# Batch 0's layers and the second attention, laid out step by step by a planner with its own list of durations

## The chip, the core and the metric

The kernel runs on one core of a Trainium2 chip. A core has a matrix engine (TensorE; PE in the profile, its weight loads PEld), VectorE (DVE), ScalarE (ACT), GpSimd (POOL), and SyncE (SP), which here only issues DMAs. Each engine works through its own list of instructions in order and waits on semaphores for the others. The metric is the device time of one execution in microseconds (us), the median over several.

## The reference

Linear attention over 4 batches of 8 heads, 576 positions, 64 dimensions, followed by two feed-forward networks on the 2304 x 512 result:

```python
def phi(x):                                   # x: q or k, w_phi: 64 x 128
    proj = np.einsum('bhsd,df->bhsf', x, w_phi)
    proj = proj - np.max(np.abs(proj), axis=-1, keepdims=True)
    return np.concatenate([np.exp(proj), np.exp(-proj)], axis=-1)
kv = np.einsum('bhsf,bhsd->bhfd', phi(k), v)
num = np.einsum('bhsf,bhfd->bhsd', phi(q), kv)
den = np.einsum('bhsf,bhf->bhs', phi(q), phi(k).sum(axis=2))[..., None] + 1e-06
x = (num / den) laid out as 2304 x 512
h = x @ w_in;  x = np.maximum(0.01 * h, h) @ w_out          # 512 -> 2048 -> 512
g = x @ w_gate                                              # 512 -> 1536
y = (g / (1 + np.exp(-g)) * (x @ w_val)) @ w_out2           # 1536 -> 512
```

The weights come in as 64-bit floats.

## The kernel before

A batch is 576 tokens, worked on as two halves of 288 columns. A layer is cut into *units*: an L1 unit makes 128 of the 2048 hidden rows ("1", f), a gate or val unit 128 of the 1536 ("g", f and "v", f), an out unit adds four such blocks into one of four 128-row blocks of the result. Every product is taken as three matmuls, since an operand is split in a high part and a low rest: (xh, wi high), (xl, wi high), (xh, wi low) at L821 (`in_ops`), and the same with gp and wo at L869 (`u_out`). All of them are recorded at L816 (`products`). A half of an input unit is 12 matmuls.

Each weight block of 128 x 512 passes through a chain the first time it is needed: a 512 KB DMA of the 64-bit words into a wi tile (L675), on ScalarE the magnitude (L691), the low bits (L694) and, for some, the sign (L697), on VectorE the shift and sign (L701, or L707 and L711) and the rounding (L719), which gives 32-bit floats in wr. These are stored to DRAM for the later batches (kept<-wr, L725). Then ScalarE rounds the high part into a wi or wo tile (L737) and VectorE subtracts the rest (L78). From batch 1 on, wr<-kept loads replace the chain's first part. There are 5 wi, 5 wo, 4 wr, 5 gp and 4 pm buffers.

An opening (the list OPENING, L41) writes batch 0's attention and the first weights out as one fixed order. After it, batch 0's units run in the order of `units`; weights are taken ahead by `split_next` (L1228), and the steps of batch 1's attention are strewn between the units by `spread` (L1242). There the tile scheduler sets the order on each engine; instructions stamped with one token keep their order. Key steps of an attention: kT load (raw, L155), projection (L207), largest (L212), two exponentials (L218, L219), product with the values (L248). Query steps: qT load, split into high and low (pk, L90 and L78), projection (L366, L367), column maxima (L370), turn (L388), the row of maxima (L394 to L406), its subtraction on PE (L420), two exponentials (L430, L436), the product with kv (L459), the denominator (L465), its reciprocal (L476 to L484) and the division (L492). Batch 2's keys go through a split of their own (pk<-raw) before their projection.

## Time and profile before

| | |
|---|---|
| three runs | 1053.72, 1054.14 (median), 1057.67 us |
| profiled execution | 1054.82 us, of which the span of its instructions 1052.9 us |
| busy in the span | PE 98%, PEld 97%, DVE 75%, ACT 62%, POOL 2% |
| granted clock of TensorE | 1.00 in every stretch shown (2.4 GHz) |
| opening | up to about 51 us |
| batch 0's layers with batch 1's attention | about 51 to 321 us |

An engine's line in a view gives its instructions' own durations; two neighbours overlap in part, so what an instruction holds its engine for is the step from its start to the next one's start. The ends of matmuls are modelled. A wait is shown in brackets behind the instruction that ended it, with the engine and line it waited for.

### The profile page before, as it was taken

How to read it: one execution, taken by the hardware profiler on the slowest of the kernel's cores; microseconds unless marked ns; L12 is line 12 of the kernel's file. 1: busy time of each engine (PE TensorE's matmuls, PEld its weight loads, DVE VectorE, ACT ScalarE, POOL GpSimd, SP SyncE). 2: the span in 40 equal slices, each digit the busy share in tenths (PEclk: the TensorE clock that was granted, in tenths of full speed). 3: DMA queues.
4: the chain of work that ended last, by engine and by line, in shares of the span. 5: the costliest groups of instructions: out<-in, count | busy, mean ns of one | idle time of the engine just before them, and what ended most of it. 6: DMA issues, size and time to landing. Idle time of an engine off the chain costs nothing.

```text
span 1052.9 us, 20402 instructions
## 1 busy us (share of the span) xinstructions
PE 1036.7 (98%) x7638; PEld 1016.8 (97%) x7638; DVE 793.5 (75%) x1726; ACT 650.5 (62%) x1448; POOL 21.4 (2%) x57
## 2 busy tenths in 40 slices
PE   9999999999999999999999999999999999999998
PEld 7899999999999999999999989999999999999998
DVE  6988888998999799678676766868778632468464
ACT  6879887898977788456543667735443244336431
POOL 1001100000000000000000000000000000000000
PEclk9999999999999999999999999999999999999999
DMA  8239777577765998765535486356886777558542
GB/s 267 60 129 309 274 264 263 168 248 217 261 192 200 356 339 284 285 230 192 192 120 189 134 319 243 141 203 217 291 285 237 272 267 264 183 167 297 191 145 76
DMA packets 101489, 236.16 MB, mean 224 GB/s; under 512 B 19856, under 2 KB 35984, under 8 KB 101392
## 3 DMA queue, kind: packets, MB, share of 16 engines
q1 hardware_dynamic: 95888, 219.74, 60.3%
q0 software_dynamic: 4032, 14.68, 3.6%
q8 instruction: 60, 0.98, 0.4%
q10 hardware_dynamic: 1472, 0.46, 0.2%
q14 instruction: 37, 0.30, 0.1%
HBM read 169.30 MB, written 65.54 MB: 223 GB/s over the span
## 4 chain that ended last, share of the span: by engine, by line
PE 83%; DVE 6%; ACT 5%; DMA 4%; issue 1%; SPq 0%; POOL 0%; DVEq 0%; ACTq 0%; POOLq 0%
PE pm L816 55%; PE pa L942 9%; PE pm L942 5%; PE pa L459 5%; PE pa L248 2%; PE pa L260 2%; PE pa L207 2%; DMA wi<-in_w_dram 2%; ACT wr L691 1%; DMA wr<-kept 1%; ACT wi L694 1%; ACT gp L90 1%; DVE gp L78 1%; PE pm L518 1%; DVE wr L701 1%
## 5 line engine op out<-in xcount | busy, mean ns | idle before, releaser
L816 PE MATMUL pm<-xh,wi 128*128 128x288 f32 x1664 | 350.5, 298 | 1.4 <-ACT wi L737 1.2
L816 PE MATMUL pm<-gp,wo 128*128 128x288 f32 x2256 | 338.4, 296 | 2.8 <-DVE acc L883 2.3
L816 PEld LDWEIGHTS pm<-gp,wo 128*128 128x128 f32 x2256 | 311.9, 188 | 4.8 <-DVE acc L883 3.0
L816 PEld LDWEIGHTS pm<-xh,wi 128*128 128x128 f32 x1664 | 271.1, 188 | 3.2 <-ACT wi L737 1.4
L816 PE MATMUL pm<-xl,wi 128*128 128x288 f32 x832 | 246.2, 297 | 0.0
L816 PEld LDWEIGHTS pm<-xl,wi 128*128 128x128 f32 x832 | 156.1, 188 | 0.8
L883 DVE TENSOR_TENSOR acc<-pm,acc 128x288 f32<-128x288 f32 x160 | 70.0, 452 | 47.2 <-PE pm L816 46.4
L78 DVE TENSOR_TENSOR gp<-es,gp 128x576 fp32r<-128x576 f32 x94 | 70.6, 752 | 31.8 <-ACT gp L90 31.0
L90 ACT ACTIVATE gp<-es 128x576 fp32r<-128x576 f32 x94 | 64.8, 694 | 29.9 <-DVE es L864 24.9
L78 DVE TENSOR_TENSOR wi<-wr,wi 128x512 fp32r<-128x512 f32 x96 | 64.7, 683 | 12.1 <-ACT wi L737 11.5
L737 ACT ACTIVATE wi<-wr 128x512 fp32r<-128x512 f32 x92 | 58.0, 643 | 25.6 <-PE pm L816 10.8
L942 PE MATMUL pm<-xh,wi 128*128 128x288 f32 x272 | 62.6, 297 | 1.8 <-DMA wi<-parts 1.6
L78 DVE TENSOR_TENSOR fl<-ff,fh 128x512 fp32r<-128x512 f32 (+1 forms) x72 | 50.9, 712 | 12.1 <-ACT fh L90 11.8
L691 ACT ACTIVATE wr<-wi 128x512 f32<-128x512 f32 x68 | 47.9, 704 | 17.0 <-DMA wi<-in_w_dram 7.8
L719 DVE TENSOR_TENSOR wr<-wr,wi 128x512 uint16<-128x512 uint16 x68 | 51.1, 754 | 0.8
L942 PEld LDWEIGHTS pm<-xh,wi 128*128 128x128 f32 x272 | 46.3, 188 | 2.9 <-DMA wi<-parts 1.8
L694 ACT ACTIVATE wi<-wi 128x512 int32<-128x512 uint32 x68 | 47.8, 703 | 0.0
L90 ACT ACTIVATE fh<-ff 128x512 fp32r<-128x512 f32 (+1 forms) x72 | 47.2, 665 | 0.8
L844 ACT ACTIVATE es<-pm 128x288 f32<-128x288 f32 x72 | 29.8, 431 | 25.4 <-PE pm L942 15.9
L465 ACT ACTIVATE dn<-pa 64x288 f32<-64x288 f32 x64 | 26.0, 407 | 30.5 <-PE pa L459 29.5
L90 ACT ACTIVATE acc<-pm 128x288 f32<-128x288 f32 x64 | 26.7, 433 | 26.3 <-PE pm L816 26.0
L864 DVE SCALAR_TENSOR_TENSOR es<-pm,es 128x288 f32<-128x288 f32 x72 | 32.1, 449 | 14.3 <-PE pm L816 14.1
(214 smaller groups left out, 2068.0 us busy)
## 6 DMA issues: line engine op xcount, KB each, us to landing
wo<-parts SPq DMA_DIRECT2D x77, 512.0 KB, 6.2
wi<-parts SPq DMA_DIRECT2D x68, 512.0 KB, 5.6
parts<-wi SPq DMA_DIRECT2D x56, 512.0 KB, 4.9
wi<-in_w_dram SPq DMA_DIRECT2D x44, 512.0 KB, 5.0
wr<-kept SPq DMA_DIRECT2D x64, 256.0 KB, 4.8
parts<-wo POOLq DMA_DIRECT2D x28, 512.0 KB, 5.2
kept<-wr SPq DMA_DIRECT2D x40, 256.0 KB, 4.5
wi<-in_wg_dram SPq DMA_DIRECT2D x12, 512.0 KB, 4.6
```

The costliest lines, as they stand in the source:

```text
L78: keep(dve.tensor_tensor(out=o, in0=a, in1=b, op=ALU.subtract))
L90: keep(act.activation(o, a, AF.Copy))
L459: keep(pe.matmul(ps, w, x, start=(i == 0), stop=(i == len(ops) - 1)))
L691: after_opening(act.activation(t[0], high.bitcast(F32), AF.Abs, scale=REBIAS))
L694: after_opening(act.activation(low, low.bitcast(U32), AF.Copy, scale=2.0**-29))
L719: keep(dve.tensor_tensor(out=t16, in0=t16, in1=e16, op=ALU.add))
L737: i = act.activation(t[:, 0], r, AF.Copy)
L816: m = pe.matmul(ps, w, x[:, c], start=(i == 0), stop=(i == n - 1))
L844: act.activation(o, i, AF.Prelu, alpha=0.01)
L864: dve.scalar_tensor_tensor(out=g[:, c], in0=ps, scalar=0.5, in1=g[:, c], op0=ALU.mult, op1=ALU.mult)
L883: dve.tensor_tensor(out=acc[o][:, t], in0=ps, in1=acc[o][:, t], op=ALU.add)
L942: m = pe.matmul(ps, a, b, start=start and n == 0, stop=stop and n == 5, skip_group_check=True)
```

## The change

A planner is added. `plan()` makes one job for each step of batch 0's units 0 to 59, of the weight chains that they need, and of batch 1's whole attention; also for the opening's last steps (TAIL, cut off OPENING), the stores kept<-wr, and the loads. A job has a cost name, the jobs it needs, the buffers it takes and uses, and a due time that follows from PE's order. `lay_out` is a list scheduler: due times are handed back from the last job to the first, then each engine takes, of the jobs that can begin first, the one due first. COSTS holds for each step how long it occupies its engine and when its result is there; a load is counted at 330 GB/s, behind the loads before it, and 1.9 us more. The jobs are emitted in that order and stamped with the opening's token. Units 60 to 63 (gate and val 10 and 11) and all behind them are left to the old way; their four weight blocks are converted in the plan without a due time of their own and stay in wi tiles.

The weights of L1, gate and val in the plan go to fh and fl tiles (3 of each) instead of wi. The split of the constants (wbd, wst), which stood beside the opening, becomes two planned jobs. `w_load` beyond those of the plan begins after unit 60. The arithmetic is the same and so are the counts of the instructions of each engine, but for the order.

```diff
+COSTS = {
+    "PE": {
+        "KP": (0.43, 0.60), "KB": (0.88, 1.05), "QP": (0.27, 0.43), "QT": (0.08, 0.30), "QS": (0.13, 0.30),
...
+    "SP": {"LD": (0.42, 1.9)},
...
+SIGNAL, RATE, FAR = 0.08, 330.0, 1.0e9
...
+def lay_out(jobs, clocks, slots, live, stay):
...
+        if j.engine in ("DVE", "ACT"):
+            j.due = min(j.due, begin.get(j.engine, FAR) - j.hold)
+            begin[j.engine] = j.due
...
+            first = min(t for t, _ in can)
+            t, j = min((c for c in can if c[0] <= first + 0.03), key=lambda c: c[1].due)
+            for u, k in can:
+                if u < t + j.hold and k.due < min(j.due, u + k.hold):
+                    t, j = u, k
...
+        if j.size:
+            moved = max(moved, t + j.hold) + j.size / RATE / 1e3
+            j.end = moved + j.result
...
-    def split_constants():
-        again = T([P, 2, F], F32, "es", 5)
-        nc.sync.dma_start(out=again.rearrange("p h f -> p (h f)"), in_=w_phi)
-        dve.tensor_copy(wbd_h, again)
...
     def parts_tile(key):
+        if in_plan[0] and key[0] in "1gv" and key not in used_later:
+            wtile[key] = t = T([P, 512], F32R, "fh", 3), T([P, 512], F32R, "fl", 3)
+            return t
...
+    UP = bounds[0][2] - 4
+    first_keys = [k for i in range(-1, UP) for k in slots[i]]
+    used_later.update(k for i in range(UP, UP + 4) for k in need[i])
...
+            ld = job("LD", call(w_load, key), [later(conv_of[first_keys[n - 5]] if n > 4 else None), round_by.get(n - 5)], [("wi", r)], size=524288)
+            ca = job("CA", call(step, 0), [ld] + [low_by[m] for m in [n - 4] if m in low_by], [("wr", w)], [r])
...
+            if kind in "1gv":
+                job("LD", call(store_f32, key), [cf], (), [w], size=262144)
...
+        nextk = job("LD", call(load_k, 2, 0), [later(qn_of[2 * NP - 1, 1])], [("raw", ("k", 2, 0))], size=294912 + 327680)
...
+        for i in range(UP):
+            for j in pes[i]:
+                j.due, now = now, now + j.hold
+            for j in at.get(i, []):
+                j.due, now = min(j.due, now), now + j.hold
...
-    for b in range(B - 1):
+    for b in range(1, B - 1):
         first, mid, end = bounds[b]
-        if b == 0:
-            mid -= 4
...
-    conv[0] = done[0] = 4
-    split_constants()
-    opening[0] = False
-    for i in range(NU):
+    in_plan[0] = True
+    for j in plan():
+        j.fn()
+    opening[0] = in_plan[0] = False
+    loaded[0] = conv[0] = done[0] = len(first_keys)
+    for i in range(UP, NU):
```

Three places show how the order moves. The first is VectorE's list ahead of the last of the four groups of out units behind batch 0's L1 (the additions acc<-pm at L883, which free pm banks for PE). Before:

```order
L701 SCALAR_TENSOR_TENSOR wr_2494<-wr_2494,wi_2299 128x512
L78 TENSOR_TENSOR wi_2445<-wr_2392,wi_2445 128x512
L719 TENSOR_TENSOR wr_2494<-wr_2494,wi_2299 128x512
L370 TENSOR_REDUCE cst_sb<-pa_2567 128x9
L701 SCALAR_TENSOR_TENSOR wr_2539<-wr_2539,wi_2346 128x512
L883 TENSOR_TENSOR acc_1068<-pm_2360,acc_1068 128x288
L883 TENSOR_TENSOR acc_1068<-pm_2374,acc_1068 128x288
```

And of the change, at the same additions (there L1473, with L865 the rounding, L847 the shift and sign, L202 the subtraction):

```order
L847 SCALAR_TENSOR_TENSOR wr_2354<-wr_2354,wi_2254 128x512
L202 TENSOR_TENSOR pk_2184<-raw_2064,pk_2184 64x576
L202 TENSOR_TENSOR gp_2416<-es_2396,gp_2416 128x576
L202 TENSOR_TENSOR pk_2241<-raw_2064,pk_2241 64x576
L1473 TENSOR_TENSOR acc_1100<-pm_2411,acc_1100 128x288
L865 TENSOR_TENSOR wr_2354<-wr_2354,wi_2254 128x512
L1473 TENSOR_TENSOR acc_1135<-pm_2429,acc_1135 128x288
L847 SCALAR_TENSOR_TENSOR wr_2402<-wr_2402,wi_2262 128x512
```

Before, five instructions for weights and a query stand in a row ahead of the first addition; in the change one weight step at most stands between neighbouring additions of this group.

The second place is the middle of batch 1's queries. SyncE's list before, with the one load of batch 2's keys (raw<-in_kT) that lies there:

```order
L725 DMA kept_3230<-wr_3224 128x512
L155 DMA raw_4838<-in_kT_dram 128x576
L675 DMA wi_3235<-in_w_dram 128x1024
L725 DMA kept_3341<-wr_3335 128x512
L675 DMA wi_3275<-in_wv_dram 128x1024
```

And of the change:

```order
L879 DMA kept_3432<-wr_3251 128x512
L821 DMA wi_3459<-in_w_dram 128x1024
L821 DMA wi_3544<-in_w_dram 128x1024
L299 DMA raw_3608<-in_kT_dram 128x576
L299 DMA raw_4470<-in_kT_dram 128x576
L299 DMA raw_4870<-in_kT_dram 128x576
L299 DMA raw_5273<-in_kT_dram 128x576
```

On ScalarE, the split of such keys is pk<-raw (L90), and a query's two exponentials are ff<-pa (L430, L436). Before:

```order
L465 ACTIVATE dn_3408<-pa_3405 64x288
L737 ACTIVATE wi_3358<-wr_3335 128x512
L430 ACTIVATE ff_3411<-pa_3187 128x288
L436 ACTIVATE ff_3411<-pa_3187 128x288
L430 ACTIVATE ff_3547<-pa_3191 128x288
L436 ACTIVATE ff_3547<-pa_3191 128x288
```

And of the change (L220 is the rounding to the high part, L576 and L582 the exponentials):

```order
L220 ACTIVATE pk_4336<-raw_3608 128x576
L576 ACTIVATE ff_3508<-pa_3434 128x288
L582 ACTIVATE ff_3508<-pa_3434 128x288
L608 ACTIVATE dn_3512<-pa_3500 64x288
L220 ACTIVATE pk_4696<-raw_4470 128x576
L608 ACTIVATE dn_3512<-pa_3504 64x288
```

Only the first of the four key loads has a job in the plan; the scheduler has brought the loads of all four forward into the planned stretch, and their splits stand between the exponentials of the queries. A third split (pk_5115<-raw_4870) stands eight rows on, directly ahead of the exponentials ff_3569, and its load raw_4870 waits for VectorE's pk_4337<-raw_3608, which frees the raw buffer.

The third place is the end of the plan, VectorE's list from the first half of unit 60 (es<-es,pm at L857 is the gate's product, es<-pm,es at L864 the val's). Before:

```order
L857 SCALAR_TENSOR_TENSOR es_4009<-es_4009,pm_4010 128x288
L78 TENSOR_TENSOR xl_3901<-xf_3897,xh_3900 128x288
L78 TENSOR_TENSOR wi_3999<-wr_3978,wi_3999 128x512
L857 SCALAR_TENSOR_TENSOR es_4009<-es_4009,pm_4025 128x288
L701 SCALAR_TENSOR_TENSOR wr_4040<-wr_4040,wi_3885 128x512
L864 SCALAR_TENSOR_TENSOR es_4009<-pm_4051,es_4009 128x288
L476 STREAM_TRANSPOSE t_855_4106<-dn_4007 128x288
L719 TENSOR_TENSOR wr_4040<-wr_4040,wi_3885 128x512
L864 SCALAR_TENSOR_TENSOR es_4009<-pm_4065,es_4009 128x288
```

And of the change, from the same product on (L1011):

```order
L1011 SCALAR_TENSOR_TENSOR es_4141<-es_4141,pm_4142 128x288
L847 SCALAR_TENSOR_TENSOR wr_4110<-wr_4110,wi_4055 128x512
L865 TENSOR_TENSOR wr_4110<-wr_4110,wi_4055 128x512
L202 TENSOR_TENSOR wo_4104<-wr_4063,wo_4104 128x512
L202 TENSOR_TENSOR gp_4119<-es_4049,gp_4119 128x576
L202 TENSOR_TENSOR gp_4043<-es_3818,gp_4043 128x576
L1011 SCALAR_TENSOR_TENSOR es_4141<-es_4141,pm_4157 128x288
L202 TENSOR_TENSOR wi_4130<-wr_4110,wi_4130 128x512
L202 TENSOR_TENSOR wi_4124<-wr_4004,wi_4124 128x512
L202 TENSOR_TENSOR wi_4127<-wr_4085,wi_4127 128x512
```

The low parts of units 61 to 63 (wi_4127, wi_4124, wi_4130), which were spread before, stand in a block at the end of the plan. On PE, unit 60's second half (12 matmuls into pm_4157) and eight high-part matmuls of units 61 and 62 lie between the matmul that ends pm_4142 and the first that reads wi_4124's low part.

## Rows read from the trace of the kernel before

**Rows 1.** The page: the span, and PE and DVE in it.

```profile
span 1052.9 us, 20402 instructions
PE 1036.7 (98%) x7638; PEld 1016.8 (97%) x7638; DVE 793.5 (75%) x1726; ACT 650.5 (62%) x1448; POOL 21.4 (2%) x57
```

**Rows 2.** Busy time by stretch: window, PE, PEld, DVE, ACT, POOL, clock, DMA share, GB/s.

```profile
300.00:350.00 50.00, 50.00 (x381) 49.79 (x380) 45.95 (x100) 38.63 (x90) 2.13 (x4) 1.00 0.67 237
...
50.00:307.50 257.50, 252.00 (x1806) 243.19 (x1805) 231.28 (x489) 219.64 (x487) 15.28 (x32) 1.00 0.69 232
```

**Rows 3.** Timeline of PE, 80 to 288 us: start, duration, instruction, [idle before it].

```profile
80.00 1.22 PE L248 MATMUL pa<-pk,ff 128*128 128x128 f32 x8 [0.43 <-POOL pk L165]
...
82.39 0.41 PE L816 MATMUL pm<-xh,wi 128*128 128x288 f32 x1 [1.18 <-ACT wi L737]
...
189.78 3.44 PE L816 MATMUL pm<-gp,wo 128*128 128x288 f32 x24 [1.75 <-DVE acc L883]
...
226.13 1.24 PE L459 MATMUL pa<-ff,kvh 128*128 128x288 f32 x4 [0.70 <-ACT ff L436]
...
287.34 3.84 PE L816 MATMUL pm<-gp,wo 128*128 128x288 f32 x27 [0.33 <-DVE acc L883]
```

**Rows 4.** The chain that ended last: start, length, piece.

```profile
97.94 6.36 PE pm L816 x48
...
294.77 1.94 PE pa L459 x8
```

**Rows 5.** Timeline of VectorE, just ahead of the wait at 189.78.

```profile
188.71 0.65 DVE L701 SCALAR_TENSOR_TENSOR wr<-wr,wi 128x512 int32<-128x512 int32 x1
189.28 1.54 DVE L883 TENSOR_TENSOR acc<-pm,acc 128x288 f32<-128x288 f32 x4
```

**Rows 6.** Timeline of VectorE, units 61 and 62.

```profile
310.90 0.77 DVE L719 TENSOR_TENSOR wr<-wr,wi 128x512 uint16<-128x512 uint16 x1
311.56 0.75 DVE L78 TENSOR_TENSOR gp<-es,gp 128x576 fp32r<-128x576 f32 x1
312.21 0.46 DVE L857 SCALAR_TENSOR_TENSOR es<-es,pm 128x288 f32<-128x288 f32 x1
...
313.89 0.45 DVE L864 SCALAR_TENSOR_TENSOR es<-pm,es 128x288 f32<-128x288 f32 x1
314.26 0.68 DVE L78 TENSOR_TENSOR wi<-wr,wi 128x512 fp32r<-128x512 f32 x1
314.86 0.69 DVE L701 SCALAR_TENSOR_TENSOR wr<-wr,wi 128x512 int32<-128x512 int32 x1
315.46 0.45 DVE L864 SCALAR_TENSOR_TENSOR es<-pm,es 128x288 f32<-128x288 f32 x1
```

**Rows 7.** Timeline of ScalarE, a query's exponentials and a split of keys.

```profile
245.22 0.41 ACT L430 ACTIVATE ff<-pa 128x288 f32<-128x288 f32 x1
245.53 0.41 ACT L436 ACTIVATE ff<-pa 128x288 f32<-128x288 f32 x1
...
249.51 0.68 ACT L90 ACTIVATE pk<-raw 128x576 fp32r<-128x576 f32 x1
250.09 0.66 ACT L697 ACTIVATE wi<-wi 128x512 int32<-128x512 f32 x1
```

**Rows 8.** DMA issues of the span: kind, count, KB each, median us to landing.

```profile
wi<-in_w_dram SPq DMA_DIRECT2D x44, 512.0 KB, 5.0
...
raw<-in_kT_dram SPq DMA_DIRECT2D x13, 288.0 KB, 4.2
```

**Rows 9.** The key load issued at 244.6 us (L155).

```profile
DMA to landing us min/median/max: 3.5/3.5/3.5
```

**Rows 10.** The key load issued at 279.8 us (L155).

```profile
DMA to landing us min/median/max: 6.5/6.5/6.5
```

**Rows 11.** The five weight loads issued from 290 to 330 us (L675).

```profile
DMA to landing us min/median/max: 3.4/4.0/5.8
```

**Rows 12.** Timeline of VectorE in the opening, the constants' split.

```profile
22.94 0.45 DVE L127 CAST wst_h<-wbd_h 64x128 fp32r<-64x128 f32 x2
```

More of the change, by code (lines that the diff above doesn't have):

```diff
@@ L1 @@
+import heapq
 from contextlib import ExitStack
@@ new lines, with __init__ @@
+"""
+COSTS = {
+    "PE": {
+        "KP": (0.43, 0.60), "KB": (0.88, 1.05), "QP": (0.27, 0.43), "QT": (0.08, 0.30), "QS": (0.13, 0.30),
+        "QN": (0.97, 1.13), "MM": (0.396, 0.56),
+        "Q4": (0.47, 0.68),
+    },
+    "DVE": {
[5 rows of a table added]
+    },
+    "ACT": {
[4 rows of a table added]
+    },
+    "SP": {"LD": (0.42, 1.9)},
+    "POOL": {"PD": (0.70, 1.9)},
+}
+COST = {name: (engine,) + cost for engine, costs in COSTS.items() for name, cost in costs.items()}
+SIGNAL, RATE, FAR = 0.08, 330.0, 1.0e9
+class Job:
+    def __init__(self, cost, fn, needs=(), takes=(), uses=(), due=FAR, at=0.0, size=0):
+        self.engine, self.hold, self.result = COST[cost]
+        self.fn, self.due, self.at, self.size = fn, due, at, size
+        self.needs = [n if isinstance(n, tuple) else (n, 0.0) for n in needs if n is not None]
+        self.takes, self.uses = list(takes), [key for _, key in takes] + list(uses)
+        self.next, self.left, self.start, self.end = [], 0, None, None
@@ L83, in keep, with planned @@
         if opening[0]:
+            tc.stamp_issue_order_token(i.ins, "opening")
+    in_plan = [False]
+    def planned(i):
+        if in_plan[0]:
             tc.stamp_issue_order_token(i.ins, "opening")
@@ L152, in load_k, with load_keys @@
     def load_k(b, j):
+        load_keys(b, j)
+        if whole(b):
+            for s in range(0, NST, 2):
+                load_values(b, j, s)
+        else:
+            vraw[b, j] = t = T([P, NST, 2, D], F32, "vraw", 1)
+            nc.sync.dma_start(out=t, in_=vt[b, j])
+    def load_keys(b, j):
         raw["k", b, j] = t = T([P, S], F32, *(("pk", 5) if b == 0 and j > 1 else ("raw", 2)))
         if b or j:
-            nc.sync.dma_start(out=t, in_=kT[b, j])
+            planned(nc.sync.dma_start(out=t, in_=kT[b, j]))
         else:
@@ new lines, in mm_out, with end_l1 @@
+    def mm_out(kind, f, o, state, t, n):
+        w, c, oc = wtile["2" if kind == "1" else "3", 0, f], slice(HT * t, HT * t + HT), slice(P * o, P * o + P)
+        if n == 0:
+            state[t] = T([P, 512], F32, "pm", 4, psm)[:, 0:HT]
+        a, d = gp[kind, 0, f]
+        for i, (part, v) in enumerate(((0, a), (0, d), (1, a))):
+            keep(pe.matmul(state[t], w[:, part, oc], v[:, c], start=n == 0 and i == 0, stop=n == CH - 1 and i == 2))
+    def end_l1(f, state, t):
+        if t == 0:
+            grown["1", f] = T([P, S], F32, "es", 5)
+        lrelu(grown["1", f][:, HT * t : HT * t + HT], state[t])
```

569 lines of the change are left out of this document (488 added, 81 removed), and 9 rows, old and new, of the table COSTS.

## The prediction

> **What bounds the kernel now.** First the page: PE is busy 98% of the span [rows 1], so a gain can only come from time in which PE waits. Then the table by stretch: from 50 to 307.5 us, the part that the change lays out anew, PE is idle 257.5 - 252.0 = 5.5 us, and from 300 to 350 us not at all; the clock is 1.00 in both [rows 2]. A matmul is shown as 0.30 us long but the next one starts 0.1325 us on (6.36/48, [rows 4]), so each stop hides 0.17 us more; with 15 to 25 stops the stretch loses some 8 to 9 us in all. That is the ceiling of what a better order can give there. Third PE's timeline with the waits in brackets: 0.43 and 1.18 us at 80 to 82 us, 1.75 at 189.78, 0.70 at 226.13, 0.33 at 287.34 [rows 3]. They have different causes (a weight's high part on ScalarE, an addition on VectorE, a query's exponentials), but all are one engine's list standing in the wrong order for a moment. The one at 189.78 shows it: the addition that frees PE's bank starts at 189.28 right behind a weight step, L701, of 188.71 [rows 5], and five such steps stand ahead of the four additions. No engine is short of time over the stretch: VectorE is busy 231 of 257.5 us, ScalarE 220 [rows 2].
>
> **What the change takes away.** The named stops are 4.4 us, with 0.17 for each of the five 5.2. In the changed order the additions of the last L1 group have at most a weight step or two between them, and the weights' high parts are placed by due times, so I count all of these as gone. The stops up to 75 us I leave as they are: the first steps of the plan are the opening's own tail. In the opening the casts of the constants no longer stand on VectorE between a query's steps; the visible pair is 0.45 us [rows 12], and a query's chain waits behind it, so up to 0.5 us is gained there; I take 0.5. Together **5.7 us off**. If the plan's durations hold everywhere it is the whole 8 to 9.
>
> What could be late next at 80 us: the first out units need four wo low parts and gp low parts that the plan leaves until just before, some eleven VectorE steps of 0.60 to 0.65 us [rows 6] in a row. They are 7 us against as much PE work; I take 1.0 us lost, with 0 and 2.0 as bounds.
>
> **The queries of batch 1: key loads brought forward.** The planner counts only one load of batch 2's keys, but the scheduler has put four into the planned stretch, with their splits between the exponentials that PE waits for. Instructions of one engine run in order, so an exponential waits for a DMA here. First split: its load is fourth in SyncE's list behind a store that waits for VectorE's rounding of wr_3251, which ends one gp step (0.65, [rows 6]) ahead of the matmul that projects the query before. From that ending: 6.5 us to landing if it is as for the key load that stood behind others [rows 10], 3.5 as for the lone one [rows 9]. Then the split 0.58 (249.51 to 250.09) and two exponentials 0.31 + 0.41 [rows 7], 1.3 together: 7.8 or 4.8 us. PE has in the meantime that 0.65, 25 matmuls of 0.1325, one small, and four fp32 products of two passes at 0.2425 (1.94/8, [rows 4]): 0.65 + 3.3 + 0.1 + 1.9 = 6.0 us. The wait is 1.8 us or none. I take 1.8, as two 512 KB loads go directly ahead. Third split: its load needs the raw buffer that VectorE's low part of the first keys frees. From the first landing: split 0.58, low part 0.65, a second landing of 4.2 (median, [rows 8]), split 0.58, exponentials 0.72, 6.7 us; PE gets through 1.3 + 3.4 (25 matmuls and a small one) = 4.7. So 2.0 us are lost; 1.3 with 3.5, 4.3 with 6.5. **3.8 us on**, bounds 0 and 7 (with the three issues ahead of the first load). In before the same stretch lists no stop of PE beside those named.
>
> The Trainium skill (DMA: Bandwidth & Descriptors, its table of fixed and variable time) fits a transfer as 2.0 us and its bytes at 436 GB/s; an estimate from it for 288 KB is 2.7 us. By it the first wait would be none and the third 0.5 us. The rows differ: the shortest of the three landings above is 3.5 and the longest 6.5, beside other traffic of 232 GB/s [rows 2], and the measurement decides.
>
> **The end of the plan, units 60 to 65.** In before this stretch has no stop at all [rows 2]. In the changed list of VectorE the low parts of units 61 to 63 stand in a block. From the end of PE's matmul into pm_4142: tanh on ScalarE 0.41 (as any 288-column step, [rows 7]), then the nine VectorE steps to the low part wi_4124: 0.37 (es), 0.60, 0.66, 0.60, 0.65, 0.65, 0.37, 0.60 by start to start and 0.68 for the last one's own time [rows 6] = 5.2. That is 5.6 us, and PE has 20 matmuls, 2.65 us. **2.9 us lost**, whatever the loads do. Behind it come weights of "3" whose loads are issued only after the plan: wi_4174 is issued behind a store that waits for the last planned rounding, 2.1 us after pm_4142; with 5.0 to landing [rows 8], three ScalarE steps of 0.58 and the three VectorE steps queued behind them (0.60, 0.60, 0.66), the product that frees the next bank ends at about 11.5, and PE needs it at 5.6 + 40 x 0.1325 = 10.9: 0.6. The next such load is issued after these, at 11.1, and its conversions stand ahead of a val product in the same way: 11.1 + 0.4 + 5.0 + 1.74 + 0.60 + 0.37 = 19.2 against PE's 11.5 + 48 x 0.1325 = 17.9: 1.3. The gp low part of unit 61 then stands behind a split of values and a rounding, some 2.3 us against 9 matmuls: 1.1. With 5.0 us a load the end of the plan costs 6.0; with 4.0, the median of the loads issued here before [rows 11], the middle two vanish and it is 4.0. With 6.5 (as [rows 10]) it is 9. I take **5.0 on**, midway between the two medians.
>
> **Sum.** -5.7 + 1.0 + 3.8 + 5.0 = +4.1 us, and I take 0.5 off because PE that has been held up gives the other engines time for the next step: +3.6. Against the profiled execution's 1054.82 us (0.68 above the median of the runs) it is 1058.4; against the median 1054.14 it is **1057.7 us**, 0.3% slower. Under 0.5%, 5.3 us, a measurement of this kernel can hardly be told from no change: the limits are 1048.9 and 1059.4.
>
> **Rivals.** (1) *The plan works and its seams are covered.* VectorE and ScalarE come to both places early, and loads land in 3.4 to 3.5 us [rows 9, 11]. Then the gain is the whole 8 to 9 us, and only the block of low parts remains, 2.9 less what VectorE is ahead: 1054.1 - 8.5 + 1 to 3 gives 1046.5 to 1048.5, faster. For it: 26 us of slack on VectorE over the stretch [rows 2]. Against it: the block starts at a product that depends on PE itself, so being early doesn't help, and the order of the hoisted splits is fixed. (2) *The loads go in bursts and come late.* Each wait on a freshly issued load is paid at 6.5 us [rows 10]: 2.8 + 4.3 at the queries, 9 at the end of the plan, 2.0 at 80 us: 18 on, 5.7 off, 1066; with only one of the two places so, about 1061. It decides from 5.5 us a load on. For it: the planner issues loads in groups (four of keys and two weights in a row), the core's DMA share is already 0.69 [rows 2]. Against: most landings in this stretch are 3.4 to 5.8 [rows 11]. (3) *Short landings, nothing else.* The loads land fast, as the lone one did, so that at the queries 1.3 remains (third split alone), at the end 4.0, at 80 us 1.0: 6.3 on, 5.7 off: no change, 1054.7. The skill's fit, named above, would make it a little better still.
>
> **How the numbers follow.** The forecast, with its own range of 1055 to 1061, has 0.42, of which 0.30 lies within 0.5% and 0.12 above; rival 1 has 0.15 (0.13 beyond the limit, 0.02 within it), rival 2 0.25, all slower, rival 3 0.18, all no change. So 0.13 for faster, 0.50 for no measurable change, 0.37 for slower. The range for 8 in 10 runs from 1048.5, where rival 1 begins, to 1063.5, short of rival 2 in full.
>
> **What would show it.** In the profile after: no stop of 1 us or more near 82 and 189 us; in ScalarE's waits pk<-raw on DMA raw<-in_kT, and near 245 to 260 us PE waiting for ff exponentials (L576, L582) or for VectorE behind them; near 310 to 330 us PE waiting first for VectorE's low part L202 (some 3 us), then for L1011 or L1018. If PE is busy throughout from 300 to 330 us, the largest term of the sum is wrong and the kernel is faster. If the stops at 189 and 226 us are still there, the plan's durations don't hold, and it is slower than I say. If batch 1's layers, 330 to 500 us, show new stops, the order beyond the plan moved too, which I count at nothing because PE had none there and the instructions there keep their old rule.

## The result, and the profile after

The changed kernel takes 1067.63 us (median of 4 runs, 1067.23 to 1068.47), the kernel before 1055.41 in the same comparison: 1.0115 times the time, interval 1.0092 to 1.0139. It is slower, by more than three times what was forecast (12.2 us against 3.6), and outside the range.

The page after, its span, its busy times and its row of the clock (in tenths, 40 slices), against [rows 1]:

```profile
span 1066.0 us, 20373 instructions
PE 1045.0 (98%) x7638; PEld 1020.8 (96%) x7638; DVE 799.6 (75%) x1726; ACT 655.2 (61%) x1448; POOL 21.6 (2%) x57
...
PEclk9999999999998999999999999999999999999999
```

Each engine runs as many instructions as before, and VectorE and ScalarE are busy only 6.1 and 4.7 us more; 13.1 us of span were added, in which PE waits or runs slowly. One slice of the clock reads 8. The windows after, with the columns of [rows 2], say where:

```profile
300.00:350.00 50.00, 46.07 (x327) 45.26 (x327) 42.38 (x84) 30.31 (x59) 2.13 (x4) 0.93 0.70 241
50.00:307.50 257.50, 250.69 (x1763) 238.37 (x1763) 230.60 (x487) 219.16 (x481) 14.95 (x31) 1.00 0.65 224
...
320.00:322.00 2.00, 0.95 (x7) 0.71 (x6) 2.00 (x4) 0.08 (x1) 0.53 (x1) 0.72 0.83 246
322.00:324.00 2.00, 1.64 (x6) 1.29 (x7) 1.47 (x3) 0.00 (x0) 0.00 (x0) 0.50 0.76 218
324.00:326.00 2.00, 2.00 (x11) 2.00 (x10) 0.00 (x0) 1.84 (x4) 0.00 (x0) 0.50 1.04 415
326.00:328.00 2.00, 2.00 (x11) 2.00 (x11) 2.00 (x4) 0.78 (x2) 0.00 (x0) 0.57 0.44 170
328.00:330.00 2.00, 2.00 (x17) 2.00 (x17) 1.63 (x4) 0.93 (x2) 0.35 (x1) 1.00 0.96 301
```

From 300 to 350 us PE had no idle time before; now 3.9 us. In addition the clock is at its lower level (0.50, 1.2 GHz) from 320.9 to 327.7 us, and 11 matmuls start in 2 us there instead of 15 or 17: the busy column shows nothing of that.

To place the loss, PE's list is walked in both traces and the usual step of each kind of matmul (the median from its start to the next start, in that trace) is added up as *work*; then the times are compared at which the same work is done. After against before the difference is:

| work done, us | 60 | 100 | 150 | 180 | 230 | 250 | 270 | 290 | 295 | 300 | 340 | 1015 |
|---|---|---|---|---|---|---|---|---|---|---|---|---|
| time before, us | 68.9 | 111.1 | 161.8 | 193.9 | 245.8 | 265.7 | 285.6 | 306.3 | 311.2 | 316.3 | 356.2 | 1039.9 |
| after, later by, us | -0.1 | -0.6 | -0.7 | -2.6 | -2.3 | 1.3 | 4.0 | 5.2 | 5.3 | 12.3 | 12.3 | 11.4 |

So 2.3 us are gained up to the work of 230, 7.5 lost from there to 290, and 7.1 within a step of 5 us of work at the plan's end. Behind it little happens. Below, "at the work of" means this table's first row. The table tells where time goes, to about 1 us: each trace has usual steps of its own, so a row drifts, and its last column is too small. Matmul against matmul (the n-th of PE's list against the n-th before, behind the plan, where both lists run in nearly the same order) the delay is 12.7 us at 342 us and 13.2 at the end.

**First loss, 240 to 275 us.** PE's stops there, start, duration, instruction and the wait in brackets:

```profile
264.95 0.40 PE L512 MATMUL pa<-pk,wst_h 128*128 128x288 f32 x1 [1.12 <-ACT ff L582]
...
268.44 0.53 PE L566 MATMUL pa<-mrow,sel 128*128 128x288 f32 x2 [0.85 <-DVE mrow L552]
...
270.35 1.97 PE L602 MATMUL pa<-ff,kvh 128*128 128x288 f32 x7 [0.58 <-ACT ff L582]
```

And on ScalarE, directly ahead of the first of them, the split that the forecast spoke of:

```profile
263.62 0.68 ACT L220 ACTIVATE pk<-raw 128x576 fp32r<-128x576 f32 x1 [1.74 <-DMA raw<-in_kT_dram]
264.20 0.39 ACT L576 ACTIVATE ff<-pa 128x288 f32<-128x288 f32 x1
```

That looks like the forecast: a split of batch 2's keys that waits for its load, and a projection of a query that waits for the exponentials behind it. But these are 2.6 us of 7.5. By the steps of PE's list, 24 matmuls between 240 and 275 us start over 0.1 us late, 6.7 us in all (4 and 0.9 before); 8 of them are row-of-maxima subtractions (L566), 7 projections (L512, L513), 6 products with kv (L602). It is the queries' whole chain that PE waits for. Why shows in the windows of one step, the division that ends a query group (two instructions each) and frees its pa banks. Window, DVE busy and count, clock, DMA share, GB/s. Before (L492):

```profile
180.00:210.00 30.00, 0.90 (x2) 1.00 0.57 199
210.00:240.00 30.00, 1.79 (x4) 1.00 0.76 252
240.00:270.00 30.00, 0.89 (x2) 1.00 0.69 211
```

After (L635):

```profile
180.00:210.00 30.00, 0.00 (x0) 1.00 0.53 187
210.00:240.00 30.00, 0.89 (x2) 1.00 0.69 239
240.00:270.00 30.00, 4.42 (x10) 1.00 0.47 167
```

Five of the eight groups end within 30 us instead of one. Each engine still has time left there (VectorE is busy 26.80 us of these 30, ScalarE 24.62), but one query's steps depend on each other.

**Second loss, the end of the plan.** PE, with the first matmuls at the lower clock and those where it comes back:

```profile
319.61 0.40 PE L968 MATMUL pm<-xh,wi 128*128 128x288 f32 x1 [2.52 <-ACT wi L220]
...
321.72 0.61 PE L968 MATMUL pm<-xh,wi 128*128 128x288 f32 x1 [1.05 <-DVE es L1011]
322.12 0.44 PE L968 MATMUL pm<-xl,wi 128*128 128x288 f32 x1
322.93 0.85 PE L968 MATMUL pm<-xh,wi 128*128 128x288 f32 x2 [0.36 <-DVE wi L202]
...
327.41 0.44 PE L968 MATMUL pm<-xl,wi 128*128 128x288 f32 x1
327.65 0.60 PE L968 MATMUL pm<-xh,wi 128*128 128x288 f32 x3
328.09 0.29 PE L968 MATMUL pm<-xl,wi 128*128 128x288 f32 x1
```

VectorE at the same place; this is the block that the order showed:

```profile
317.82 0.73 DVE L847 SCALAR_TENSOR_TENSOR wr<-wr,wi 128x512 int32<-128x512 int32 x1
318.65 0.74 DVE L865 TENSOR_TENSOR wr<-wr,wi 128x512 uint16<-128x512 uint16 x1
319.29 0.68 DVE L202 TENSOR_TENSOR wo<-wr,wo 128x512 fp32r<-128x512 f32 x1
319.88 1.42 DVE L202 TENSOR_TENSOR gp<-es,gp 128x576 fp32r<-128x576 f32 x2
321.22 0.45 DVE L1011 SCALAR_TENSOR_TENSOR es<-es,pm 128x288 f32<-128x288 f32 x1
321.58 1.89 DVE L202 TENSOR_TENSOR wi<-wr,wi 128x512 fp32r<-128x512 f32 x3
```

ScalarE's largest wait from 300 to 330 us (total, times, longest):

```profile
ACT wr L837 <- DMA wi<-in_w_dram: 4.1, 1, 4.1
```

Of the 7.1 us, 2.8 are late starts up to 320 us. Of the 4.35 behind it, 1.4 are the two stops at 321.72 and 322.93; the remaining 2.9 are matmuls at the lower clock: from 323.81 to 327.65 sixteen start 0.24 us apart instead of 0.1325, which alone is 1.7. The clock fell at 320.9 us, when PE had the stop of 2.52 and the first 0.2 us of the next one behind it. The high part that ended the first stop was begun on ScalarE at 318.93, behind eight other steps that it works through without a gap from 315.03 on; the load in the last fence landed 4.2 us after its issue, and no later stop of PE waits for it.

### The profile page after: what moved, and what is told of

Read it like the earlier page. It is cut to its first block, busy times and chain, and to the rows that moved or that the text cites. A ratio compares the mean times of both kernels' runs of the same rounds, so it can differ in the third digit from the quotient of the medians.

```text
span 1066.0 us, 20373 instructions
## 1 busy us (share of the span) xinstructions
PE 1045.0 (98%) x7638; PEld 1020.8 (96%) x7638; DVE 799.6 (75%) x1726; ACT 655.2 (61%) x1448; POOL 21.6 (2%) x57
## 4 chain that ended last, share of the span: by engine, by line
PE 76%; DVE 9%; ACT 6%; DMA 6%; issue 2%; SPq 0%; POOL 0%; DVEq 0%; ACTq 0%; POOLq 0%
PE pm L968 42%; PE pa L1096 9%; PE pm L1096 5%; PE pm L1427 4%; PE pm L1437 4%; PE pa L602 4%; PE pa L386 2%; PE pa L398 2%; DMA wi<-parts 2%; DVE wr L865 1%; ACT wr L837 1%; DMA wi<-in_w_dram 1%; PE pa L347 1%; PE pm L661 1%; DVE xl L202 1%
## 5 line engine op out<-in xcount | busy, mean ns | idle before, releaser
L968 PE MATMUL pm<-xh,wi 128*128 128x288 f32 x1088 | 228.4, 298 | 3.9 <-ACT wi L220 2.5
L968 PEld LDWEIGHTS pm<-xh,wi 128*128 128x128 f32 x1088 | 178.6, 190 | 4.8 <-ACT wi L220 2.7
L968 PE MATMUL pm<-xl,wi 128*128 128x288 f32 x544 | 161.0, 297 | 0.0
L968 PEld LDWEIGHTS pm<-xl,wi 128*128 128x128 f32 x544 | 103.0, 189 | 0.0
L202 DVE TENSOR_TENSOR gp<-es,gp 128x576 fp32r<-128x576 f32 x94 | 70.4, 752 | 27.3 <-ACT gp L220 26.5
L220 ACT ACTIVATE gp<-es 128x576 fp32r<-128x576 f32 x94 | 64.5, 686 | 27.7 <-DVE es L1018 22.6
L1427 PE MATMUL pm<-xh,fh 128*128 128x288 f32 x256 | 79.0, 309 | 0.0
L1427 PE MATMUL pm<-xh,fl 128*128 128x288 f32 x256 | 75.6, 295 | 0.0
L1427 PE MATMUL pm<-xl,fh 128*128 128x288 f32 x256 | 75.5, 295 | 0.0
L1096 PE MATMUL pm<-xh,wi 128*128 128x288 f32 x272 | 62.6, 297 | 2.6 <-DMA wi<-parts 2.1
L202 DVE TENSOR_TENSOR fl<-ff,fh 128x512 fp32r<-128x512 f32 (+1 forms) x72 | 51.1, 713 | 11.8 <-ACT fh L220 11.4
L865 DVE TENSOR_TENSOR wr<-wr,wi 128x512 uint16<-128x512 uint16 x68 | 50.6, 756 | 1.1
L202 DVE TENSOR_TENSOR wi<-wr,wi 128x512 fp32r<-128x512 f32 x64 | 43.0, 685 | 9.4 <-ACT wi L893 5.9
L1096 PEld LDWEIGHTS pm<-xh,wi 128*128 128x128 f32 x272 | 46.3, 188 | 3.6 <-DMA wi<-parts 2.5
L1427 PEld LDWEIGHTS pm<-xh,fh 128*128 128x128 f32 x256 | 48.3, 189 | 0.9 <-DVE es L1455 0.3
L1427 PEld LDWEIGHTS pm<-xl,fh 128*128 128x128 f32 x256 | 48.1, 188 | 0.5
```

Source lines behind the costliest of these rows:

```text
L202: keep(dve.tensor_tensor(out=o, in0=a, in1=b, op=ALU.subtract))
L220: keep(act.activation(o, a, AF.Copy))
L865: keep(dve.tensor_tensor(out=t16, in0=t16, in1=e16, op=ALU.add))
L968: m = pe.matmul(ps, w, x[:, c], start=(i == 0), stop=(i == n - 1))
L1096: m = pe.matmul(ps, a, b, start=start and n == 0, stop=stop and n == 5, skip_group_check=True)
L1427: keep(pe.matmul(state[t], part(w, i)[:, r], v[0, kt][:, c], start=kt == 0 and n == 0, stop=kt == KD - 1 and n == 2))
```

## The experiments

Runs of 3 rounds, of 5 for e10_tail, e11_sig15, e12_fx, e12_fx8 and the three of the last section; in parentheses the median of the kernel before on the same chip. Two kernels of different chips are compared by their ratios.

### The key loads and the four weights

*e1_due* gives the four weights that units 60 to 63 need a due time:

```diff
+        for n, i in enumerate(range(UP, UP + 4)):
+            for key in need[i]:
+                for j, _ in [(conv_of[key], 0.0), split_of[key][1]]:
+                    j.due = now + 3.2 * n
```

> The high and low parts of the four weights of units 60 to 63 get due times (the end of the plan, 3.2 us apart). Theory A, that their block at the end of the plan causes the stop at 317 to 323 us and, through it, the stretch at half the clock: both go, some 6 of the 7.1 us lost there, about 1061.5 us. Rival B, that the loads issued only after the plan set that stop: PE still waits 3 us or more near 320 us and the clock still falls, 1064 to 1067 us.

1072.00 us (1057.00), ratio 1.0137 [1.0112, 1.0163]. Neither expectation came. The loss at the plan's end grows: +5.5 us at the work of 290, +13.5 at 295, +17.4 at 310. PE now waits for the products of units 58 to 60 instead, which have no due time either and come behind the dated weights:

```profile
320.44 0.58 PE L968 MATMUL pm<-xh,wi 128*128 128x288 f32 x1 [6.10 <-DVE es L1451]
...
337.02 0.40 PE L968 MATMUL pm<-xh,wi 128*128 128x288 f32 x1 [1.76 <-DVE es L1011]
```

*e2_keys* keeps batch 2's key loads and splits behind the plan:

```diff
-        if b or j:
+        if b == 2:
+            after_opening(nc.sync.dma_start(out=t, in_=kT[b, j]))
+        elif b or j:
...
+        opening[0] = b == 2
         cp(h, r)
         sub(l, r, h.bitcast(F32))
+        opening[0] = False
```

> The loads and splits of batch 2's keys are stamped so that they come after the plan on their engines (only the one load that the plan has stays in it). Theory A, that the exponentials wait behind those splits: the stops at 264.95 and 270.35 us go and 4 to 5 us of the time lost between 243 and 279 us come back, 1062.5 to 1063.5 us. Rival C, that VectorE has no time left there and the splits only ride along: 1 us or less, 1066.5 us or more. The end of the plan is as before, with its 7 us.

1064.37 us (1057.00), ratio 1.0066 [1.0046, 1.0086]. This lies between the two expectations. At the work of 290 it is +1.6 instead of +5.2: the splits cost 3.6 us, or 2.3 if only the way from 230 to 290 is counted. But from 230 (-3.5) to 290 (+1.6) 5.2 of the 7.5 us are still lost with no key split in the way: the larger part has another cause.

*e3_both* has both edits.

> Both edits: due times for the last four weights, and batch 2's keys after the plan. If the two terms are separate (theory A) they add up: about 10.5 us, 1057 us, with what is left over the kernel before from smaller stops at 290 us and in the middle. If one hides the other (rivals B, C) it is 1062 us or more.

1066.26 us (1057.00), ratio 1.0084 [1.0055, 1.0114]. The two edits don't add up. +2.5 at 290, +9.7 at 295, by one stop, again for an undated product of VectorE; six weight steps fill the time of the stop ahead of it, and the window 312 to 322 us around it has the clock at 0.66:

```profile
315.26 0.58 PE L972 MATMUL pm<-xh,wi 128*128 128x288 f32 x1 [4.72 <-DVE es L1455]
```

So a due time for some of the undated steps harms the others.

### The buffers of the split weights

*e5_wi* takes back the part of the change that puts the split weights in fh and fl; they go to wi tiles as before:

```diff
-        if in_plan[0] and key[0] in "1gv" and key not in used_later:
-            wtile[key] = t = T([P, 512], F32R, "fh", 3), T([P, 512], F32R, "fl", 3)
-            return t
```

> The planned kernel with its split weights of L1, gate and val in wi tiles, as in the kernel before, and not in fh and fl. Theory D, that the other buffers are what lets the loads run ahead: loads come later, more stops between 80 and 300 us, 1070 us or more. Rival: five wi tiles are enough for a plan that knows of them, within 1.5 us of 1067.6.

1075.77 us (1057.00), ratio 1.0175 [1.0147, 1.0204], the slowest of all. +0.7 at 230, +10.4 at 270, +18.3 at 300, with two long stops:

```profile
286.57 0.37 PE L1424 MATMUL pm<-xh,wi 128*128 128x288 f32 x1 [3.72 <-DVE es L1452]
...
328.71 0.61 PE L965 MATMUL pm<-xh,wi 128*128 128x288 f32 x1 [6.40 <-ACT wi L220]
```

So the other buffers are worth 6 to 8 us to this plan; they are not where the time went.

### Due times for everything at the end, and an earlier end

*e8_alldue* is e3_both with a due time for every step behind a unit's matmuls, and for weights 8 and 9 of "3":

```diff
+            for j in behind_of[i]:
+                j.due = min(j.due, now + (1.0 if j.hold < 0.5 else 8.0))
...
+        for f in (8, 9):
+            for j in (conv_of["3", 0, f], split_of["3", 0, f][1][0]):
+                j.due = min(j.due, now + 8.0)
```

> Batch 2's keys after the plan as in e2_keys, and a due time for every step that has none: the products and splits behind the last units (1 us after their unit for a product, 8 us for a gp split), the last two weights of the 3 layer (8 us after the plan), the four weights of units 60 to 63 (3.2 us apart). Theory A2, that steps without a due time are put off or put ahead of the wrong ones at the end of the plan: the loss between PE work 290 and 300, 7.1 us in the change and 5.9 in e2_keys, falls to 2 or less, about 4 us better than e2_keys. Rival B2, that the last weights' loads come too late whatever the order: 5 us or more are still lost there.

1062.24 us (1055.70), ratio 1.0062 [1.0043, 1.0082]. The loss of 7.1 us is gone: +0.4 at 290, +0.5 at 310. From 310 to 320 4.3 us come back, in five stops of 0.32 to 0.71 us; two of them:

```profile
330.22 0.50 PE L351 MATMUL pa<-wbd_h,pk 128*128 128x256 f32 x2 [0.69 <-ACT pk L220]
...
334.41 0.79 PE L972 MATMUL pm<-gp,wo 128*128 128x288 f32 x4 [0.71 <-DVE wo L202]
```

Four of the five wait for a key split and for the "3" weights 10 and 11, which still come only after the plan; the fifth, of 0.65, is for an addition. In total it is hardly better than e2_keys, where 4 us had been expected.

*e9_half* ends the plan four units into the second half, and leaves the queries, gate and val to the old way; *e9_half_due* adds e1's due times to it:

```diff
-    UP = bounds[0][2] - 4
+    UP = bounds[0][1] + 4
...
-        for g in range(2 * NP):
+        for g in range(0):
...
+    spread(q_steps(1), UP, bounds[0][2] - 3)
```

> The plan ends behind batch 0's L1 and its out units (unit 32), with batch 1's keys in it; the queries and the gate and val units go the old way. Theory E, that the plan gains in its first half (2.6 us up to PE work 180) and loses in the second, where queries stand close together, and at its end: the gain stays, nothing is lost between 230 and 290, and it is 0 to 3 us below the kernel before. Rival F, that any end of a plan costs some 5 us, since the steps behind it are issued late: the loss moves to about 215 us and the kernel is 3 us or more above the one before.

> As e9_half, with due times for the four weights of the first units behind the plan. By A2 it is the same as e9_half or up to 2 us better, if those weights hold the plan's end up; by rival F the same as e9_half, above the kernel before.

1067.64 and 1068.18 us (1055.70), ratios 1.0113 [1.0087, 1.0140] and 1.0118 [1.0092, 1.0143]: as slow as the changed kernel. In e9_half the difference is -0.5 at 150, +4.4 at 180, +9.8 at 210. Two of its stops, for an addition and for a query's maxima; the clock falls to 0.50 with each, from 170.1 to 176.9 and from 224.7 to 228.1 us:

```profile
170.89 3.25 PE L1439 MATMUL pm<-gp,wo 128*128 128x288 f32 x12 [1.55 <-DVE acc L1475]
...
223.32 0.33 PE L534 MATMUL pa<-cst_sb 128*128 128x128 f32 x1 [3.25 <-DVE cst_sb L516]
```

The first matmul outside the plan (L970) starts at 201.2 us. So one loss, 4.9 us, lies some 30 us ahead of the plan's end, and the other, 5.4, some 20 us behind it, at a query left to the old way. The total fits a cost of the plan's end wherever it stands, the places fit only roughly, and the due times of the weights make no difference. I take nothing more from this pair than that the loss isn't bound to units 56 to 63.

*e10_tail* is e8_alldue with "3" weights 10 and 11 and batch 2's first key split taken into the plan, and gate and val 10 of the four weights put in fh and fl:

```diff
+    for i in range(UP, UP + 4):
+        for k in [k for k in slots[i] if k[0] == "3" and k[1] == 0]:
+            slots[i].remove(k)
+            slots[UP - 1].append(k)
...
+        k20 = [job("GH", call(k_high, 2, 0), [nextk], [("pk", ("k20", 0))], [("k", 2, 0)])]
+        k20.append(job("GL", call(k_low, 2, 0), k20, [("pk", ("k20", 1))], [("k", 2, 0), ("k20", 0)]))
...
+        for f in range(8, NF2):
...
+                j.due = min(j.due, now + 2.0 + 1.6 * (f - 4))
```

> e8_alldue with what still lay behind the plan brought into it: the last two weight loads of the 3 layer (32-bit conversions and all), and the split of batch 2's first keys; two of the four last gate and val weights in fh and fl. Theory G, that the 4.3 us which e8_alldue loses between PE work 310 and 320 come from those loads and that split being issued only after the plan: 1 us or less is lost there, and the kernel ends within 0.2% of the one before. Rival, that VectorE is simply behind with its work by then (the plan's own list ends on VectorE 9 us after it ends on PE): 3 us or more are lost there still.

1059.13 us (1056.82, 12 runs), ratio 1.0024 [1.0014, 1.0034]. The 4.3 us from 310 to 320 are gone. From 300 to 310 2.7 are lost, more than the 1 expected, and for other steps, the parts of the dated weights themselves:

```profile
321.03 0.53 PE L979 MATMUL pm<-xh,wi 128*128 128x288 f32 x2 [1.40 <-DVE wi L202]
...
324.35 0.40 PE L979 MATMUL pm<-xh,wi 128*128 128x288 f32 x1 [0.40 <-ACT wi L904]
```

*e11_sig15* asks whether the planner merely underrates the delay from one engine to the next; it is e10_tail with that constant doubled:

```diff
-SIGNAL, RATE, FAR = 0.08, 330.0, 1.0e9
+SIGNAL, RATE, FAR = 0.15, 330.0, 1.0e9
```

> e10_tail with 0.15 instead of 0.08 us in the plan for the way from one engine to another. Theory H, that the planned stretch slips behind its own list (1 us by 60 us, 4 us by 255) because the list allows too little between engines: with more, the loss between PE work 220 and 270 (5.9 us in e8_alldue) falls to 3 or less. Rival I, that the queries' chain itself is the limit there, whatever the list allows: the same loss within 1 us.

1061.70 us (1056.82), ratio 1.0044 [1.0027, 1.0061]: worse than e10_tail by 2.6 us. From 230 to 270 it loses 3.3 us (e10_tail 5.1), but it has less to lose, -0.6 at 230 against -3.8. Over the stretch that the expectation names, 220 to 270, with one list of usual steps for both, it loses 5.3 and e10_tail 6.2: within the 1 us of rival I. The constant is not it.

### The queries

In the plan the high and low part of a group's division get one due time for all groups (L1680), 4.4 us times the last query's place, and the division inherits it: by the planner's list divisions are due at 242 to 249 us, whichever group they end. Until then a group keeps pa banks, of which there are four: projections due at 174 us start at 211 in the list, those due at 189 at 240. *e12_fxonly* is the changed kernel with this alone mended:

```diff
-            xhj.due = xlj.due = qplaces[-1] * 4.4
+            ends_of.append((xhj, xlj, qn_of[g, 0], qn_of[g, 1]))
...
+        for high, low, *qn in ends_of:
+            high.due = low.due = max(j.due for j in qn) + 5.0
```

> The change with one edit: the division at the end of a query group, due in the plan only at the end of all queries (about 248 us), is due 5 us behind that group's own products. Theory J, that this late due time keeps the group's pa banks, so that the later query groups cannot begin and stand packed into 230 to 270 us: the packed queries spread out (products up to 290 us), the 5.6 us lost between PE work 230 and 260 fall to 1.5 or less, while the end of the plan keeps its loss of 5 to 7 us; about 1061 to 1063 us against 1067.6. Rival I, that the chain from step to step of a query sets it: 4 us or more are still lost between 230 and 290.

1061.62 us (1056.30), ratio 1.0054 [1.0032, 1.0076]. The loss from 230 to 290 is gone altogether: -1.8 at 230, -1.7 at 260, -2.0 at 290. The windows of the division, as above:

```profile
180.00:210.00 30.00, 0.90 (x2) 1.00 0.48 164
210.00:240.00 30.00, 2.65 (x6) 1.00 0.55 190
240.00:270.00 30.00, 1.75 (x4) 1.00 0.72 229
```

The edit moves the key loads as well, since the plan has the first of them behind the last query's product. They are issued from 296 to 303 us (from 259 to 267 in the changed kernel), and their splits stand behind the last exponentials:

```profile
300.33 0.69 ACT L220 ACTIVATE pk<-raw 128x576 fp32r<-128x576 f32 x1 [1.31 <-DMA raw<-in_kT_dram]
```

So by itself this run doesn't tell the packed queries from the splits among them; e2_keys and the next pair do.

At the plan's end it loses what the changed kernel loses, 6.9 us from 295 to 300, here in one stop, and with the clock down (0.66 in the window 312 to 322 us):

```profile
314.90 0.61 PE L968 MATMUL pm<-xh,wi 128*128 128x288 f32 x1 [4.87 <-ACT wi L220]
```

*e12_fx* is e10_tail with the same edit, *e12_fx8* has 8 us in place of 5.

> e10_tail with the same edit. Theory J: the 4.6 us that e10_tail gains by PE work 220 are kept to 290, and it ends 2 to 4 us below the kernel before. Rival I: as e10_tail, 1.5 us or more above the kernel before.

> The same with 8 us in place of 5. Theory J: within 1.5 us of e12_fx, since four banks leave room for one group more; if the exact number decides, the two differ by 2 us or more.

1057.44 and 1057.34 us (1056.30, 12 runs each), ratios 1.0012 [0.9999, 1.0024] and 1.0006 [0.9995, 1.0018]. In e10_tail batch 2's key splits already stood behind the queries, and e12_fx differs from it by the due time alone: e10_tail falls from -3.8 at 230 to +1.3 at 270, these two are at -2.5 to -3.0 still at 290. That is the packing without the splits, and it is the due time's. The 5 us or 8 make no difference. The totals are level with the kernel before, not the 2 to 4 us below it that were expected: both lose some 2.9 us from 300 to 310, in e12_fx8 by a stop of 1.57 us for VectorE's low part and one of 0.40.

### What is left at the plan's end: order or backlog

*e13_early* is e12_fx8 with the four weights due 5 us earlier; *e13_late* also puts off what units 60 to 63 don't need; *e14_last* is e13_late with the later due time of the gp parts for the plan's last eight units alone. The diff is e14_last's against e12_fx8; e13_early has only its first hunk, and in e13_late the second reads 13.0 for all units:

```diff
-                    j.due = now + 3.2 * n
+                    j.due = now + 3.2 * n - 5.0
...
-                j.due = min(j.due, now + (1.0 if j.hold < 0.5 else 8.0))
+                j.due = min(j.due, now + (1.0 if j.hold < 0.5 else 13.0 if i >= UP - 8 else 8.0))
...
-            j.due = now + 2.0
+            j.due = now + 6.0
...
-                j.due = min(j.due, now + 2.0 + 1.6 * (f - 4))
+                j.due = min(j.due, now + 8.0 + 1.6 * (f - 4))
```

> As e12_fx8, but the four weights of units 60 to 63 are due 5 us earlier. What is open is why PE still loses about 2.9 us at the work of 300 to 310 us (a stop of 1.57 us for a low part of VectorE, one of 0.40 for a high part of ScalarE). Theory K, the order at the plan's end: the low parts are dated too late by the plan's own lateness of some 3 to 4 us; dated 5 us earlier, the stop of 1.57 is under 0.3 us and the loss at work 310 under 1.0 us: ratio 0.998 to 0.999. Theory L, VectorE's backlog: at the end of the plan VectorE is behind by more steps than PE leaves time for, so another order moves the stop to another step of the same size: ratio 1.000 to 1.002, and the stop waits for something else of VectorE (es, acc or gp).

> As e13_early, and the steps that units 60 to 63 do not need (gp parts of the last units due at 13 us behind their products instead of 8, the weights of "3" 8 to 11 from 8 us instead of 2, batch 2's first key split from 6 us instead of 2) are dated later. Theory K: as e13_early or better, loss at work 310 under 0.5 us, ratio 0.997 to 0.999. Theory L: the postponed steps come due a few us on and stop PE there, behind 320 us of work: loss at the work of 310 small but 2 us or more again by 340; ratio 1.000 to 1.002.

> As e13_late, but the gp parts keep their due time of 8 us behind their products in all units but the last eight of the plan; in e13_late the 13 us held for all units, and PE lost 4.5 us more than e13_early between the work of 80 and 150 us, at the first out units (0.67 + 0.19 us of stops for wo's low parts). Theory K (order): the lead at the work of 180 to 290 us is back at 2 us or more, there is no stop at 300 to 340 us as in e13_late, and the ratio is 0.996 to 0.9975. Theory L (backlog): a stop of VectorE's comes back between 300 and 340 us, 1.5 us or more, and the ratio is 0.998 or above.

| | us (before), 12, 11 and 12 runs | ratio | delay at 222 us | 309 | 335 | 362 |
|---|---|---|---|---|---|---|
| e13_early | 1055.34 (1057.02) | 0.9981 [0.9969, 0.9993] | -3.0 | -1.6 | -0.5 | -0.6 |
| e13_late | 1058.62 (1057.02) | 1.0017 [1.0006, 1.0028] | -1.5 | 1.1 | 1.1 | 2.3 |
| e14_last | 1054.97 (1056.80) | 0.9983 [0.9972, 0.9995] | -3.2 | -2.1 | -1.9 | -0.8 |

The delays here are matmul against matmul, at times of the kernel before (e12_fx8: -3.3, -2.3, 1.2 and 0.9). In e13_early the stop is 0.76 instead of 1.57, which is not under the 0.3 expected. In e13_late PE has none from 300 to 340 us, but the later due time held for the first out units too: it falls 1.2 us behind e13_early from 80 to 120 us (not 4.5, as the expectation of e14_last has it, which went by steps of each trace's own), and more at the queries. Its total lies in the range of theory L, without the stop that L names. e14_last has both: the lead of the middle, and no stop at the plan's end. Its windows (columns of [rows 2]):

```profile
300.00:310.00 10.00, 10.00 (x78) 10.00 (x77) 9.94 (x22) 9.54 (x19) 0.53 (x1) 1.00 0.72 265
310.00:320.00 10.00, 10.00 (x78) 9.96 (x77) 9.96 (x22) 8.97 (x22) 0.00 (x0) 1.00 0.42 130
320.00:330.00 10.00, 10.00 (x80) 10.00 (x79) 10.00 (x19) 6.03 (x13) 1.60 (x3) 1.00 0.82 277
330.00:340.00 10.00, 10.00 (x79) 10.00 (x78) 9.04 (x24) 7.23 (x20) 0.00 (x0) 1.00 0.97 356
```

VectorE is full from 300 to 330 us and PE waits for nothing: at the place in question it was the order, not VectorE's backlog. The ratio doesn't say so: it misses the 0.996 to 0.9975 of theory K and lies where L has it. What is missing goes at one stop behind that place, 1.2 us with what it hides, at an out unit that waits for a tanh of ScalarE:

```profile
350.18 1.46 PE L979 MATMUL pm<-gp,wo 128*128 128x288 f32 x9 [0.79 <-ACT es L1009]
```

e13_late has the same stop (0.79 at 353.24), e13_early has not, and ScalarE is busy from 345 to 350 us without a gap. That the steps put off have come due there fits this, but no run shows it. Both e13_early and e14_last beat the kernel before, by 0.2%.

## Why the prediction failed

- **What bounds the kernel, and the ceiling.** Right: what the change moved is in PE's waits and in the slower matmuls behind them, and the gain stayed within 8 to 9 us. (Of the five steps ahead of the additions at 189.28 us four are for weights, the fifth is a query's.) The best lead that any variant had was 4.8 us (e8_alldue at the work of 220).
- **"5.7 us off".** The named stops [rows 3] are gone as said. The stop at 189.78 gave its 1.9 us (from -0.7 at the work of 150 to -2.6 at 180). But with the 1.0 us for the first out units, and without the stop at 287.34, the sum had 4.2 us net up to the work of 230, and 2.3 came: the 0.5 of the opening [rows 12] isn't there (-0.1 at 60), at the first out units 0.5 came in place of 1.0, and small new stops (0.48 at 217.56 for the row of maxima) took back about what 226.13 gave. I took each stop as gone and no new one in its place.
- **"3.8 us on" at the queries: the step that failed.** I read the hoisted key splits as the whole cause and put the plan's own timing of the queries at nothing. I priced two splits; the first wait, worked out by [rows 7, 10], stands in the trace (1.74 us for the load, 1.12 for PE against 1.8), the one behind the third split is 0.58 against 2.0. The loss was 7.5 us. e2_keys without the splits still loses 5.2, so the splits are 2.3 to 3.6 of it. A split term of about the right size doesn't save the sum: the larger part was not in it. e12_fxonly, which edits only the divisions' due time, loses none; e12_fx against e10_tail shows the same with the splits out of the way in both. The cause was in the change's code, one due time for all eight groups (L1680), and a bank held until then; this due time doesn't follow from PE's order, as I had written of all of them. I looked at what stood *between* a query's steps, not at *when* each query group began and ended. The count of divisions by stretch would have shown it from the order.
- **"5.0 on" at the end of the plan: place and cause right, the first wait wrong, size short.** Steps that no due time orders stop PE at the named place, first for a weight of units 61 to 63, then for L1011. The first wait is for the high part on ScalarE (2.52), which I had as ready. The low part that I priced at 2.9 comes last and costs only 0.36 more, since the stops ahead of it had used up the time. e8_alldue shows the cause: with due times for all, 7.1 us become 0.1. The late "3" weights and the key split are a term of their own (4.3 in e8_alldue, gone in e10_tail, which loses 2.7 for other weights); in the changed kernel no stop waits for them. Of the size, 2.9 of the 7.1 are matmuls at the lower clock, which I had at 1.00 throughout [rows 2]; without them it is 4.2, within 1 us of the forecast. That nearness is in part luck: the late loads and the gp part of unit 61, 3.0 of the 6.0 priced, cost PE nothing here.
- **What would show it.** Of the signs named, these came: no stop at 189 and none above 0.2 us at 82, ScalarE waiting for raw<-in_kT, PE for exponentials at 265 us, PE for L1011 and L202 at 320 to 323, and hardly a change behind 340 (12.7 us at 342 us, 13.2 at the end, matmul against matmul). One did not: PE's first wait at the plan's end is not for L202, and that for L202 is 0.36 us, not some 3.
- **The half us taken off** for PE's delay was an idea without a row; nothing shows it.
- **The rivals.** (2) comes nearest in time (1066) and named both places, but not by its mechanism: the landings of the four key loads after (minimum, median, maximum) are all short of 6.5, and one wait for them is above 1 us:

```profile
DMA to landing us min/median/max: 2.7/3.8/5.0
```

  The Trainium skill's fit of 2.7 us (DMA: Bandwidth & Descriptors, the section Anatomy of one DMA, its table of fixed and variable time; an estimate for 288 KB) is one of transfers that GpSimd issues, and SyncE issues these. The shorter of these landings, 2.7 and 2.8 us, agree with it, for loads that had no weight load directly ahead; the other two came behind two 512 KB loads and took about 5. Rival (1), that the plan works, is what e14_last is once the due times are mended, at a quarter to a third of the gain that the rival promised (1.8 us of 5.6 to 7.6).
- **Sum.** -2.3 + 7.5 + 7.1 = +12.3 at the work of 300, and 13.1 in the span of the profiled execution, against +4.1 before the half us. Of the 8.2 between, 1.9 are gains that did not come up to the work of 230, 4.2 the queries (7.5 against 3.8 less the stop at 287.34), 2.1 the end of the plan.

## What to carry to other kernels

In a list scheduler a due time is also a statement on how long buffers are held: a step that frees a scarce buffer (here a PSUM bank of four) must be due when its own group ends, or later groups, however early they are due, pack behind it. A step without a due time isn't neutral; it comes after all that have one, and dating some of such steps makes the rest later (e1_due, e3_both), so date all that the first work behind the plan needs, or none. When reading such a change blind, count one kind of step per stretch of PE's order before and after, and look for what is packed, before pricing single waits.

## What the runs showed of the hardware

Stops of PE can cost more than their own length. In the changed kernel PE stopped 2.52, 1.05 and 0.36 us between 317 and 323 us; the granted clock was 0.72 from 320 to 322, 0.50 to 326, 0.57 to 328 and 1.00 from there, while PE was busy throughout from 324 us on. It fell at 320.9 us, so the stop of 0.36 comes behind the fall. In e3_both and e12_fxonly one stop of 4.72 or 4.87 us did the same (0.66 over 312 to 322 us), and the clock fell while the stop lasted, at 313.2 and 312.3 us. In e2_keys two stops of 1.10 and 1.09 us, 0.8 us of work apart, were enough: 0.50 from 315.8 to 322.6 us. In e12_fx8, with stops of 1.57 and 0.40 us, the windows 318 to 330 us have 1.00, and so has 300 to 350 us in e8_alldue, with its five of 0.32 to 0.71 us. So the sum of the stops alone doesn't tell which of these cases it will be. A stop should be priced with what the clock does behind it; in this kernel that was 2.9 us on about 4.
